# An attention, routing and expert kernel whose first key tile is filled and loaded by other engines, and whose first scores stand behind two groups of decay products

## The chip, the cores and the metric

The kernel runs on one core of a Trainium2 chip. The metric is the device time of one execution, in microseconds (us). TensorE (PE, with its weight loads as PEld), VectorE (DVE), ScalarE (ACT), GpSimd (POOL) and the queue of SyncE (SP) each work through their own list of instructions in order, and semaphores tie the lists together.

## The reference

Three stages follow each other. The first is a gated linear attention with a running maximum, written as a loop over 768 steps for 4 x 8 = 32 heads of width 40:

```python
m_new = np.maximum(f_gate[:, :, t] + m, i_gate[:, :, t])
f_stab = np.exp(f_gate[:, :, t] + m - m_new)
i_stab = np.exp(i_gate[:, :, t] - m_new)
C = f_stab[..., None, None] * C + i_stab[..., None, None] * np.einsum('bhd,bhe->bhde', vt, kt)
n = f_stab[:, :, None] * n + i_stab[:, :, None] * kt
y[:, :, t] = o * np.einsum('bhde,bhe->bhd', C, qt) / np.maximum(np.abs(nq), 1.0)
```

Here `o` is the sigmoid of `o_gate` and `nq` is the product of `n` and `q`. The second stage sends each of the 3072 tokens (320 numbers each) to one of 8 experts, 384 tokens each, greedily by the sorted logits of `x @ w_gate`; an expert is `relu(x @ w1) @ w2` with 1024 inner columns. The third is a gated block over all tokens, `(sigmoid(x @ w_gate) * (x @ w_val)) @ w_out`, with 1536 inner columns.

## The kernel before

The attention is cut into 6 chunks of 128 time steps, and in each chunk the 32 heads go in three sets of 12, 12 and 8. A pair of chunk and set is a step j, so there are 18 steps. Within a step the heads go in groups of four, numbered k; a group is written (j, k) below. For a group, `decay` (lines 221 to 237) multiplies a mask (`tris`, L226) and the running sums of the gates (`GB` by `sel`, L228) into a PSUM tile `pg`, of which there are two, and ScalarE turns it into `ee` by four exponentials (L234). `score` (239 to 246) multiplies keys and queries on TensorE (L245) into `s`, of which there are two as well, and VectorE multiplies `ee` by it (L246). `outp` (L294) multiplies `ee` by the values, `state` (L275 and L283) carries the running matrix on, `comb` and `xout` (L307 to L322) make the output rows `y`.

The key operand of `score` is `KB`, two tiles of 120 partitions x 12 x 128 numbers. Three heads of width 40 share the 120 partitions; each head's column block has keys in its own 40 rows and zeros in the other 80. The zeros are written once, at the start of `setup`, and `load` then writes only the 40 rows of each head, by three transfers (`"k"`, L126).

The start is a chain of its own. `setup` loads the gates of the first 128 steps (L57 on SyncE's queue, L58 on ScalarE's), zeroes the two `KB` tiles on ScalarE, loads queries, values and keys of step 0, then the gates of the other 640 steps (L67, L68), then the operands of step 1. `gates(0, 1)` (151 to 193) makes the running maximum and sums of the first chunk on VectorE; its last line fills the last third of `GB` (L192), on which the first L228 waits. `gates(1, NC)` does the same for the other five chunks: a scan over 640 columns (L156), differences (L158, L170, L159), five scans (L165), and behind them an exponential on ScalarE (`lam`, L185). The sigmoid of the output gate `on` (L139) needs another activation table than the exponentials, so a table load stands before and behind each pair of sigmoids.

The attention is written in the order of `run` and `step`, but it isn't issued so: a scheduler with a model of the engines orders it, and `issue_after` holds an instruction behind a named one. From the routing on (`manual_schedule`) the order is that of the code. While the attention runs, side work splits the weights of the third stage into two parts (L774 to L776 on VectorE, L818 on ScalarE, L819 on GpSimd).

Of the kernel before, what the change touches and what calls it, by code (L numbers as in the profile page):

```python
# [14 lines left out]
AF = mybir.ActivationFunctionType  # L15
# [6 lines left out]
L = 128  # L22
# [8 lines left out]
GK = (3, 3, 2)  # L31
GP = 3 * D
# [8 lines left out]
class Attention:  # L41
# [9 lines left out]
    def setup(self):  # L51
        nc, one, g = self.nc, self.one, self.g
        gp = self.gp
        gt = self.gt = gp.tile([96, 2, S], FT, name="gt")
        gi = [self.a[n].rearrange("b h s -> (b h) s") for n in ("i_gate", "f_gate")]
        for r in range(3):
            nc.sync.dma_start(gt[32 * r:32 * r + 32, 0, :L], gi[0][:, :L])  # L57
            nc.scalar.dma_start(gt[32 * r:32 * r + 32, 1, :L], gi[1][:, :L])  # L58
        self.KN = [one.tile([L, HS, D], FT, name=f"kn{i}") for i in range(2)]
        self.VN = [one.tile([L, HS, 41], FT, name=f"vn{i}") for i in range(NS)]  # L60
        self.KB = [one.tile([GP, 4, 3, L], FT, name=f"kb{i}") for i in range(2)]
        for t in self.KB:
            nc.scalar.activation(t.rearrange("p a r t -> p (a r) t"), g["ident"][:GP, None, :].to_broadcast([GP, 12, L]),
                                 AF.Copy, scale=0.0)
        self.load(0, "qvk")
        for r in range(3):
            nc.sync.dma_start(gt[32 * r:32 * r + 32, 0, L:], gi[0][:, L:])  # L67
            nc.sync.dma_start(gt[32 * r:32 * r + 32, 1, L:], gi[1][:, L:])  # L68
        self.load(1, "kqv")
        g["R"].strict(g["jp"])  # L70
        self.KW = one.tile([L, HS, D], FT, name="kw")
        self.CS = one.tile([GP, NG, 123], FT, name="cs")
        nc.vector.memset(self.KW[:, 8:9], 0.0)
        nc.vector.memset(self.VN[2][:, 8:9], 0.0)
        nc.vector.memset(self.VN[2][:, 8:9, D:], 1.0)
        self.mk = one.tile([GP, 2, 3], FT, name="mk")
        nc.gpsimd.iota(self.mk[:, 0], pattern=[[-D, 3]], base=0, channel_multiplier=1,
                       allow_small_or_imprecise_dtypes=True)
        nc.vector.tensor_scalar(self.mk[:, 1], self.mk[:, 0], 0.0, None, op0=OP.is_ge)
        nc.vector.scalar_tensor_tensor(self.mk[:, 1], self.mk[:, 0], float(D - 1), self.mk[:, 1], op0=OP.is_le,  # L80
                                       op1=OP.mult)
        self.negi = one.tile([L, L], BF, name="negi")
        nc.vector.tensor_scalar(self.negi, g["ident"], NEG, None, op0=OP.mult)
        self.sel = one.tile([96, NB], BF, name="sel")
        it = gp.tile([96, NB], FT, name="it")
        for r in range(3):
            nc.gpsimd.iota(it[32 * r:32 * r + 32], pattern=[[1, NB]], base=0, channel_multiplier=-1,
                           allow_small_or_imprecise_dtypes=True)
        nc.vector.tensor_scalar(self.sel, it, 0.0, None, op0=OP.is_equal)
        self.m = gp.tile([96, S + 1], FT, name="m")  # L90
        self.G = gp.tile([96, S], FT, name="G")
        self.zero = gp.tile([96, 1], FT, name="zero")
        nc.vector.memset(self.zero, 0.0)
        nc.vector.memset(self.m[:, 0:1], NEG)
        self.GT = one.tile([L, NC, 96], FT, name="GT")
        self.GB = one.tile([96, S], BF, name="GB")
        self.LM = one.tile([GP, NG, NC], FT, name="LM")
        self.lam = gp.tile([32, NC], FT, name="lam")
        for _ in self.gates(0, 1):
            pass  # L100
# [10 lines left out]
    def heads(self, s):  # L111
        return s * HS, min(NB, (s + 1) * HS)

    def load(self, j, which):
        nc = self.nc
        c, s = divmod(j, NS)
        h0, h1 = self.heads(s)
        n, ng = h1 - h0, GS[s]
        for w in which:
            if w == "q":  # L120
                self.QT[j] = self.wk.tile([GP, 4, L], FT, name="qT", bufs=3)
                nc.sync.dma_start(self.QT[j][:, :ng], self.a["qt"][c, s, :, :ng])
            elif w == "k":
                for r in range(3):
                    p = slice(D * r, D * r + D)
                    nc.sync.dma_start(self.KB[j % 2][p, :ng, r, :], self.a["kt"][c, s, p, :ng])  # L126
                if c < NC - 1:
                    nc.sync.dma_start(self.KN[j % 2][:, :n], self.a["kn"][c, s, :, :n])
            else:
                nc.sync.dma_start(self.VN[s][:, :n], self.a["vn"][c, s, :, :n])  # L130
                nc.gpsimd.memset(self.VN[s][:, :n, D:], 1.0)
# [89 lines left out]
    def decay(self, j, k):  # L221
        nc = self.nc
        c, s = divmod(j, NS)
        h0 = s * HS + 4 * k
        pg = self.ps.tile([L, 4, L], FT, name="pg", bufs=2)
        nc.tensor.matmul(pg, self.g["R"].tris, self.negi[:, None, :].to_broadcast([L, 4, L]), start=True, stop=False)  # L226
        for h in range(4):
            nc.tensor.matmul(pg[:, h, :], self.sel[:, h0 + h:h0 + h + 1].to_broadcast([96, L]),  # L228
                             self.GB[:, c * L:(c + 1) * L], start=False, stop=(h == 3))
        ee = self.wk.tile([L, 4, L], FT, name="ee", bufs=7)  # L230
        ins, n = self.behind
        with self.tc.issue_after(ins) if n else nullcontext():
            for h in range(4):
                e = nc.scalar.activation(ee[:, h, :], pg[:, h, :], AF.Exp, bias=self.GT[:, c, h0 + h:h0 + h + 1])  # L234
        self.lastexp = e.ins
        self.behind[1] = max(0, n - 1)
        self.W[j, k] = ee

    def score(self, j, k):
        nc = self.nc  # L240
        ee = self.W[j, k]
        s = self.ps.tile([L, 4, L], FT, name="s", bufs=2)
        for h in range(4):
            a, r = divmod(4 * k + h, 3)
            nc.tensor.matmul(s[:, h, :], self.KB[j % 2][:, a, r, :], self.QT[j][:, a, :], start=True, stop=True)  # L245
        nc.vector.tensor_mul(ee, s, ee)  # L246
# [119 lines left out]
    def run(self, rt, fn):  # L366
        with self.tc.tile_pool(name="a_gate", bufs=1) as self.gp:
            self.setup()
            self.kw(0)
            for k in range(GK[0]):  # L370
                self.decay(0, k)
                self.score(0, k)
            gend = self.gend
            g1 = self.gates(1, NC)
            for k in range(GK[1]):
                self.decay(1, k)
            self.step(0, lambda n: [next(g1, 0) for _ in range(2 * n)])
            for _ in g1:
                pass
            self.step(1, lambda n: None)  # L380
            self.setup2()
            self.lambdas()
        with self.tc.tile_pool(name="a_conv", bufs=1) as cv:
            with self.tc.issue_after(gend):
                rt.consts(cv)
            side = fn.prep_moe2(cv)
            for j in range(2, NC * NS + 1):
                self.step(j, lambda n: [next(side, 0) for _ in range(n)])
            for _ in side:
                pass  # L390
# [363 lines left out]
class Ffn:  # L754
# [24 lines left out]
    def prep_moe2(self, wk):  # L779
# [20 lines left out]
        for t in todo[:2]:  # L800
            load(t)
# [440 lines left out]
```

## Time and profile before

| what | value |
|---|---|
| median of three runs | 851.53 us (850.21 to 854.12) |
| the profiled execution | 853.9 us, of which its span is 852.1 us |
| PE busy | 800.9 us, 94% of the span |
| DVE, ACT, POOL busy | 519.4, 334.9 and 230.2 us |
| mean granted TensorE clock | 0.973 of full speed |

The span begins with the first instruction and ends with the last; the 1.8 us beside it lie around the program. A row of a timeline gives the start and the length of a group of like instructions, the engine, the line, the tiles (out<-in) and in brackets how long the engine had sat idle before and what ended that. The attention fills the first 192 us, the routing the next 30, and the experts and the gated block the rest.

### The profile page before, as it was taken

Reading aid. Unit: us, or ns where it says so; the run is one execution under the profiler, and the core shown is the slowest. Engines: PE = TensorE matmul, PEld = TensorE weight load, DVE = VectorE, ACT = ScalarE, POOL = GpSimd, SP = SyncE. Lnnn points to the kernel's source line nnn. Section 1 sums busy time; section 2 is a strip of 40 time slices with the busy share of each in tenths; the row PEclk is TensorE's granted clock in tenths of the full one; section 3 lists DMA queues with packets and bytes.
Section 4 is the critical chain, followed back from the end, with each engine's and each line's share of the span. In section 5 each row is a group of like instructions: output and inputs, shape, how many; then the busy total and the mean of one; then the engine's idle time right before and its main releaser. Section 6 shows DMA issues by size and latency. Waiting matters only on the chain.

```text
span 852.1 us, 15713 instructions
## 1 busy us (share of the span) xinstructions
PE 800.9 (94%) x6049; PEld 761.2 (89%) x6049; DVE 519.4 (61%) x1381; ACT 334.9 (39%) x751; POOL 230.2 (27%) x253
## 2 busy tenths in 40 slices
PE   6888899994799999999999999999999999999996
PEld 5787888893599999999999999999999999999996
DVE  7689989856576576656565665566566652352321
ACT  5565697620342342252334224322522342252321
POOL 2144544410210270081026005400810270072001
PEclk9898999996699999999999999999999999999998
DMA  6586676410400410310051005002200400320000
GB/s 184 172 264 204 209 237 210 133 44 32 132 29 2 144 40 1 104 58 24 2 145 37 3 2 159 24 1 83 78 24 2 144 32 8 94 67 24 1 1 23
DMA packets 40949, 67.64 MB, mean 79 GB/s; under 512 B 5066, under 2 KB 29386, under 8 KB 40874
## 3 DMA queue, kind: packets, MB, share of 16 engines
q1 hardware_dynamic: 38426, 58.72, 22.7%
q0 software_dynamic: 2304, 7.87, 2.8%
q8 instruction: 47, 0.77, 0.4%
q14 instruction: 28, 0.23, 0.1%
q10 hardware_dynamic: 144, 0.05, 0.0%
HBM read 58.76 MB, written 7.86 MB: 78 GB/s over the span
## 4 chain that ended last, share of the span: by engine, by line
PE 72%; DVE 2%; DMA 1%; ACT 0%; issue 0%; POOL 0%; POOLq 0%; ACTq 0%; DVEq 0%
PE mm L1003 8%; PE mm L1025 8%; PE mm L1004 8%; PE mm L1005 8%; PE mm L1010 5%; PE mm L1009 5%; PE ac L1129 5%; PE ac L1131 5%; PE ac L1130 5%; PE ac L1042 3%; PE ac L1044 3%; PE ac L1043 3%; PE rp L611 3%; PE ac L1048 1%; DMA xg<-xd,ix 1%; PE ac L1047 1%
## 5 line engine op out<-in xcount | busy, mean ns | idle before, releaser
L1003 PE MATMUL mm<-yh,mh 128*128 128x384 f32 x384 | 134.0, 349 | 0.0
L1004 PE MATMUL mm<-yh,ml 128*128 128x384 f32 x384 | 129.3, 337 | 0.0
L1005 PE MATMUL mm<-yl,mh 128*128 128x384 f32 x384 | 129.3, 337 | 0.0
L963 POOL DMA_INDIRECT xg<-xd,ix x24 | 23.6, 985 | 371.7 <-DVE scr L730 274.8
L1105 DVE TENSOR_TENSOR gl<-gf,gh 128x384 fp32r<-128x384 f32 x96 | 77.6, 808 | 38.9 <-ACT gh L1111 38.7
L1098 ACT ACTIVATE sg<-mm 128x384 f32<-128x384 f32 x96 | 47.1, 490 | 135.7 <-PE mm L1010 133.7
L1111 ACT ACTIVATE gh<-gf 128x384 fp32r<-128x384 f32 x96 | 50.2, 523 | 109.0 <-DVE gf L1110 109.0
L1129 PE MATMUL ac<-oh,gh 128*128 128x320 f32 x282 | 90.6, 321 | 0.0
L1110 DVE TENSOR_TENSOR gf<-sg,mm 128x384 f32<-128x384 f32 x96 | 52.7, 549 | 60.0 <-ACT sg L1098 59.3
L1131 PE MATMUL ac<-oh,gl 128*128 128x320 f32 x282 | 87.4, 310 | 0.7 <-DVE gl L1105 0.7
L1130 PE MATMUL ac<-ol,gh 128*128 128x320 f32 x282 | 87.4, 310 | 0.0
L1033 ACT ACTIVATE gh<-mm 128x384 fp32r<-128x384 f32 x64 | 31.3, 491 | 115.9 <-PE ac L1048 52.7
L1003 PEld LDWEIGHTS mm<-yh,mh 128*128 128x128 f32 x384 | 72.6, 189 | 0.2 <-DVE xl L944 0.2
L1004 PEld LDWEIGHTS mm<-yh,ml 128*128 128x128 f32 x384 | 72.7, 189 | 0.0
L1005 PEld LDWEIGHTS mm<-yl,mh 128*128 128x128 f32 x384 | 72.3, 188 | 0.0
L1010 PE MATMUL mm<-pad,mr 128*128 128x384 f32 x192 | 64.9, 338 | 0.0
L1009 PE MATMUL mm<-y,m 128*128 128x384 f32 x192 | 64.6, 336 | 0.0
L245 PE MATMUL s<-qT,kb 120*128 120x128 f32 x384 | 57.2, 293 | 2.5 <-DVE ee L246 1.7
L245 PEld LDWEIGHTS s<-qT,kb 120*128 120x128 f32 x384 | 50.6, 203 | 8.5 <-DVE GT L183 4.3
L234 ACT ACTIVATE ee<-pg,GT 128x128 f32<-128x128 f32 x192 | 53.7, 381 | 11.4 <-PE pg L228 9.9
L294 PE MATMUL po<-vn,ee 128*128 128x123 f32 (+2 forms) x384 | 52.6, 287 | 4.3 <-DVE ee L246 4.2
L1034 DVE SCALAR_TENSOR_TENSOR gl<-mm,gh 128x384 fp32r<-128x384 f32 x64 | 34.6, 551 | 33.9 <-ACT gh L1033 33.4
(295 smaller groups left out, 1898.2 us busy)
## 6 DMA issues: line engine op xcount, KB each, us to landing
ws<-in_moe_w_dram SPq DMA_DIRECT2D x15, 480.0 KB
ws<-in_moe_w_dram SPq DMA_DIRECT2D x14, 512.0 KB
ws<-in_moe_w_dram SPq DMA_DIRECT2D x18, 256.0 KB
on<-in_on_dram SPq DMA_DIRECT2D x6, 640.0 KB
xd<-y SPq DMA_DIRECT2D x24, 160.0 KB
st<-in_moe_w_out_dram SPq DMA_DIRECT2D x12, 320.0 KB
st<-in_moe_w_gate_dram SPq DMA_DIRECT2D x8, 384.0 KB
st<-in_moe_w_val_dram SPq DMA_DIRECT2D x8, 384.0 KB
```

Source lines behind the costliest of these rows:

```text
L234: e = nc.scalar.activation(ee[:, h, :], pg[:, h, :], AF.Exp, bias=self.GT[:, c, h0 + h:h0 + h + 1])
L245: nc.tensor.matmul(s[:, h, :], self.KB[j % 2][:, a, r, :], self.QT[j][:, a, :], start=True, stop=True)
L1003: mm(p, wh[:, d, cs], h[:, d], start=(d == 0), stop=False)
L1004: mm(p, wl[:, d, cs], h[:, d], start=False, stop=False)
L1005: mm(p, wh[:, d, cs], l[:, d], start=False, stop=False)
L1009: mm(p, w2[:, cs], x[2], start=False, stop=False)
L1010: mm(p, wr[:, c2], self.pad[z], start=False, stop=True)
L1025: mm(p, (self.al if t == 1 else self.ah)[:, d, cs], x[t // 2][:, d], start=(d == 0 and t == 0), stop=False)
L1105: nc.vector.tensor_tensor(gl, hs[f - 1][0], hs[f - 1][1].bitcast(FT), op=OP.subtract)
L1129: mm(o, gh[:, ts], self.oh[:, k], start=(k == 0), stop=False)
L1130: mm(o, gh[:, ts], self.ol[:, k], start=False, stop=False)
L1131: mm(o, gl[:, ts], self.oh[:, k], start=False, stop=(k == 11))
```

## The change

Two engines take over the zero fills: VectorE zeroes the first `KB` tile and GpSimd the second. `load` gets an optional engine for the key transfers, and the first call passes ScalarE, whose queue then issues the three key transfers of step 0; in that call keys (with the `kn` rows) come first, then queries, then values. `decay` returns its last matmul. In `run`, the groups (0, 0) and (0, 1) of decay products come first, and all scores of step 0, with the decay group (0, 2), are held behind the last matmul of group (0, 1).

```diff
-        for t in self.KB:
-            nc.scalar.activation(t.rearrange("p a r t -> p (a r) t"), g["ident"][:GP, None, :].to_broadcast([GP, 12, L]),
-                                 AF.Copy, scale=0.0)
-        self.load(0, "qvk")
+        nc.vector.memset(self.KB[0], 0.0)
+        nc.gpsimd.memset(self.KB[1], 0.0)
+        self.load(0, "kqv", nc.scalar)
...
-    def load(self, j, which):
+    def load(self, j, which, keng=None):
...
-                    nc.sync.dma_start(self.KB[j % 2][p, :ng, r, :], self.a["kt"][c, s, p, :ng])
+                    (keng or nc.sync).dma_start(self.KB[j % 2][p, :ng, r, :], self.a["kt"][c, s, p, :ng])
...
-            nc.tensor.matmul(pg[:, h, :], self.sel[:, h0 + h:h0 + h + 1].to_broadcast([96, L]),
+            mm = nc.tensor.matmul(pg[:, h, :], self.sel[:, h0 + h:h0 + h + 1].to_broadcast([96, L]),
                              self.GB[:, c * L:(c + 1) * L], start=False, stop=(h == 3))
...
+        return mm.ins
...
-            for k in range(GK[0]):
-                self.decay(0, k)
-                self.score(0, k)
+            self.decay(0, 0)
+            mm = self.decay(0, 1)
+            with self.tc.issue_after(mm):
+                self.score(0, 0)
+                self.decay(0, 2)
+                for k in range(1, GK[0]):
+                    self.score(0, k)
```

The scheduler places the whole attention anew, so the order also differs at many places behind the start. Lines of the changed program stand one lower from L66 to L238 (L228 is L227), as before up to L369, and four higher behind that.

The first place is the start of TensorE's list. Before, eight score products of two groups (`kb_99` is the first key tile) stand ahead of the first products of `sel` and `GB`:

```order
L226 MATMUL pg<-negi,tris 128x512
L182 MATMUL tr<-ident,gt 128x96
L245 MATMUL s<-qT,kb_99 128x128 x8
L228 LDWEIGHTS sel
L228 MATMUL pg<-GB,sel 128x128
...
L275 MATMUL pic<-vn_96,kw 120x123 x4
```

With the change it reads:

```order
L225 MATMUL pg<-negi,tris 128x512
L181 MATMUL tr<-ident,gt 128x96
L227 LDWEIGHTS sel
L227 MATMUL pg<-GB,sel 128x128
...
L245 MATMUL s<-qT,kb_99 128x128 x8
L275 MATMUL pic<-vn_96,kw 120x123 x3
```

The eight products of `sel` that complete two `pg` tiles now stand ahead of the eight scores.

The second place is on TensorE too, some 25 us into the program, where the mask product of group (3, 0) stands. It needs a `pg` tile that is free only when the exponentials of group (2, 0) are done. Before, it stands ahead of the scores of group (1, 2) (`kb_100` is the second key tile) and of the first eight value products of step 1 (`vn_97`):

```order
L182 MATMUL tr<-ident,gt 128x96 x4
L226 LDWEIGHTS tris
L226 MATMUL pg<-negi,tris 128x512
L245 MATMUL s<-qT,kb_100 128x128 x4
L294 MATMUL po<-vn_97,ee 128x123 x8
```

With the change these rows read:

```order
L245 MATMUL s<-qT,kb_100 128x128 x4
L294 MATMUL po<-vn_97,ee 128x123 x8
L275 MATMUL pic<-vn_97,kw 120x123
L245 MATMUL s<-qT,kb_99 128x128
L225 LDWEIGHTS tris
L225 MATMUL pg<-negi,tris 128x512
```

Scores and value products have moved ahead of the mask product of group (3, 0), and the four transposes of the gates ahead of them all.

The third place is the start of SyncE's queue. Before:

```order
L130 DMA vn_96<-in_vn_dram 128x492
L128 DMA kn_94<-in_kn_dram 128x480
L67 DMA gt<-in_i_gate_dram 32x640
L126 DMA kb_99<-in_kt_dram 40x4x128 x3
L68 DMA gt<-in_f_gate_dram 32x640
L67 DMA gt<-in_i_gate_dram 32x640
```

With the change:

```order
L127 DMA kn_94<-in_kn_dram 128x480
L121 DMA qT<-in_qt_dram 120x512
L129 DMA vn_96<-in_vn_dram 128x492
L66 DMA gt<-in_i_gate_dram 32x640
L67 DMA gt<-in_f_gate_dram 32x640
```

The three key transfers have left this queue, and all six transfers of the later gates (`gt`) follow directly on the operands of step 0. On ScalarE's list the three key transfers stand behind its own three gate transfers and ahead of the first table load, and the exponential `lam` of the five later chunks stands behind 12 exponentials where it stood behind 20; the sigmoids stand behind 24 exponentials in both.

## Rows read from the trace of the kernel before

**Rows 1.** The page: span, and granted TensorE clock in 40 equal slices.
```profile
span 852.1 us, 15713 instructions
PEclk9898999996699999999999999999999999999998
```

**Rows 2.** Who waited for whom on PE, 0 to 230 us: total us, times, longest.
```profile
PE pg L226 <- ACT ee L234: 6.1, 4, 4.2
```

**Rows 3.** Timeline of the start: start us, us, engine line op out<-in xcount [idle before <-releaser].
```profile
0.84 0.09 DVE L73 MEMSET kw<- 128x40 f32 x1 [0.84 <-PEq L1229]
...
0.94 0.06 DVE L94 MEMSET m<- 96x1 f32 x1
...
1.82 0.16 POOL L105 MEMSET wgt<- 128x80 f32 x1
...
3.46 2.86 ACT L63 ACTIVATE kb<-ident 120x1536 f32<-120x1536 f32 x2
...
3.65 0.48 DVE L156 TENSOR_TENSOR_SCAN m<-gt,m 96x128 f32<-96x128 f32 x1 [1.42 <-DMA gt<-in_f_gate_dram]
...
4.97 2.62 SPq L126 DMA_DIRECT2D kb<-in_kt_dram  x3
...
7.81 0.90 DVE L192 CAST GB<-G 32x128 bf16<-32x128 f32 x1
7.84 4.03 PE L245 MATMUL s<-qT,kb 120*128 120x128 f32 x16 [0.84 <-ACT GT L184]
...
9.55 0.42 SPq L68 DMA_DIRECT2D gt<-in_f_gate_dram  x1
...
11.58 1.55 DVE L156 TENSOR_TENSOR_SCAN m<-gt,m 96x640 f32<-96x640 f32 x1 [1.88 <-DMA gt<-in_f_gate_dram]
...
11.70 0.61 PE L228 MATMUL pg<-GB,sel 96*128 96x128 bf16 x8
...
12.13 5.26 ACT L234 ACTIVATE ee<-pg,GT 128x128 f32<-128x128 f32 x20 [4.60 <-PE pg L228]
```

**Rows 4.** The same view, 15 to 30 us.
```profile
15.38 0.38 PE L226 MATMUL pg<-negi,tris 128*128 128x512 bf16 x1 [0.43 <-ACT ee L234]
...
16.40 1.16 PE L245 MATMUL s<-qT,kb 120*128 120x128 f32 x8 [0.42 <-DVE ee L246]
...
17.25 0.83 SPq L135 DMA_DIRECT2D on<-in_on_dram  x2
...
19.16 0.21 ACT L185 ACTIVATE lam<-G 32x5 f32<-32x5 f32 x1 [1.77 <-DVE G L165]
...
24.82 0.49 PE L182 MATMUL tr<-ident,gt 96*128 96x96 f32 x4
...
25.70 1.27 ACT L139 ACTIVATE on<-on 128x1280 f32<-128x1280 f32 x1 [0.90 <-DMA on<-in_on_dram]
...
26.99 1.28 ACT L234 ACT_TABLE_LOAD   x1
...
28.29 1.14 ACT L234 ACTIVATE ee<-pg,GT 128x128 f32<-128x128 f32 x4
...
29.48 0.59 PE L226 MATMUL pg<-negi,tris 128*128 128x512 bf16 x1 [4.16 <-ACT ee L234]
```

**Rows 5.** Busy us by stretch (times in brackets are instructions), granted clock, DMA share, GB/s.
```profile
8.00:12.00 4.00, 4.00 (x22) 3.71 (x23) 2.05 (x15) 0.00 (x0) 0.63 (x1) 1.00 0.46 140
...
30.00:31.00 1.00, 1.00 (x7) 1.00 (x6) 0.00 (x0) 0.84 (x4) 0.01 (x1) 0.50 0.78 287
...
35.00:36.00 1.00, 1.00 (x8) 0.91 (x7) 0.00 (x0) 0.00 (x0) 0.00 (x0) 0.76 0.96 309
...
60.00:80.00 20.00, 16.58 (x121) 15.19 (x120) 19.93 (x41) 11.04 (x37) 9.84 (x11) 0.83 0.65 197
```

**Rows 6.** Timeline again: the end of the cold stretch, and a later stall.
```profile
38.00 0.61 PE L228 MATMUL pg<-GB,sel 96*128 96x128 bf16 x8
...
74.31 2.07 PE L294 MATMUL po<-vn,ee 128*128 128x123 f32 x8 [2.54 <-DVE ee L246]
```

## The prediction

> **What bounds the kernel now.** I read the page first. Span and clock slices [rows 1] say that TensorE runs at full clock from about 240 us on, where the order of work is the code's own and this change touches nothing. What can move lies in the attention, the first 192 us, where the clock slices dip for the first time in the second slice (21 to 43 us). So I asked who waits for whom on TensorE up to 230 us. One wait stands out: the mask product of a decay group waits for exponentials, 6.1 us in four waits, the longest 4.2 us [rows 2]. The timeline places it: TensorE finishes the gate transposes at 25.3 us and resumes at 29.48 [rows 4]. ScalarE is what ends it, with a chain of its own: the second transfer of `on` lands at 25.70, its sigmoid takes 1.27, the table goes back for 1.28, and four exponentials run from 28.29 for 1.14 [rows 4]. Behind the wait the granted clock is 0.50, the lower of the two levels (1.2 GHz), up to the stretch from 35 to 36 us, where it is 0.76 [rows 5]. So the idle time is paid twice, once as waiting and once as slow matmuls. Third I read the start [rows 3]. ScalarE, which must make 24 exponentials before those sigmoids, sits idle for 4.60 us until the first decay products come at 12.13, because TensorE works through 16 score passes (4.03 us) first. VectorE waits 1.88 us for the last of the later gates, landed at 11.58. Both delays feed the chain that ends at 29.48.
>
> **The fills.** ScalarE's two fills, 2.86 us [rows 3], go. ScalarE had nothing else to do then, so that alone is worth nothing. VectorE now starts with a fill of 1536 numbers per partition. No row shows one so long. Two small fills, 0.09 us for 40 numbers and 0.06 us for one [rows 3], give a slope of 0.77 ns and a lower bound of 1.2 us; 0.09 us over 40 gives 2.3 ns and an upper bound of 3.5 us. I take 1.4 us, half of ScalarE's 2.86 for two tiles of this very shape, the nearest row in size. Cover: VectorE's small work from 0.84 us ends 1.42 us before the gates land at 3.65 [rows 3], so a fill of 1.4 us just fits, and the chain behind it moves by about 0.2 us (with 3.5 us, by 2.1). GpSimd's fill stands ahead of the small index rows that VectorE needs before the scan; 0.16 us for 80 numbers [rows 3] bounds it at 3.1 us, and with that the chain moves by 1.3 us. I take 0.2 us for both and keep 2.1 as the far end; a gain from these two edits is excluded, since nothing they do starts earlier. The Trainium skill, "VectorE: DVE Perf Modes", section "Zero memsets can be issued as uint32 (trn2)", says that a memset takes one cycle per element whatever the type; at that page's 0.96 GHz this would be an estimate of 1.6 us, the chain would move by 0.4 us in place of 0.2, and the sum below would be 0.2 us smaller. No row here shows a fill of that length.
>
> **The key transfers.** SyncE spends 2.62 us on issuing them from 4.97 [rows 3], and the later gates stand behind. ScalarE now issues them from about 2.3 to 4.9 us, then loads its table (1.28 us, the price of the row at 26.99 [rows 4]), done at 6.2; its first real work on the path is the exponential that released the scores at 7.84 [rows 3]. So nothing is late there. The last gate transfer, issued at 9.55 and landed at 11.58, so 2.0 us later [rows 3], is issued some 3.4 us sooner (2.6 of issue, 0.8 of waiting for the fill) and lands at about 8.2. VectorE is free for it at about 9.8, so the long scan starts about 1.7 us earlier, and so does `lam`, 17.4 in place of 19.16 [rows 4]. The twelve exponentials that now stand behind `lam` then end at about 20.7, as the 24th does now, so no loss comes from the new place of `lam`. The transfers of `on`, issued at 17.25 now [rows 4], have fewer bytes ahead of them: the operands of step 1 leave SyncE 3.4 us sooner. I put the second landing at 23 us or before, and the end of sigmoids and table load at 26.2 in place of 28.29.
>
> The 16 DMA engines are busy 0.46 of the time from 8 to 12 us [rows 5], so the issue and not the movement is what the gates wait for. The Trainium skill, "DMA: Bandwidth & Descriptors", section "Issuing engines are not separate DMA queues", says that all queues run on the same 16 engines and that a second queue saves only the time of issuing. By that rule a full set of engines would land the gates no sooner, and the sum below would be -3.2 in place of -6.2; the share of 0.46 says they are not full.
>
> **TensorE, as a sum up to the eight `sel` products that end at 38.61** [rows 6]. I take away and add, in its own time:
>
> - The wait of 4.16 us before 29.48 [rows 4] goes: minus 4.2. Two things remove it, and either would nearly do. The exponentials come 2.1 us sooner, and four scores and eight value products, which now run behind the wait, stand ahead of it. At full clock those are 3.2 us of work: eight score passes take 1.16 [rows 4], and the 16 value passes, 2.07 for eight at half clock [rows 6], about 1.0 for each eight.
> - The slow clock goes with it. From 29.48 to 35 us it is at half, and 0.76 in the sixth microsecond [rows 5]: 6.0 us at the lower level, of which half is lost: minus 3.0.
> - Three small waits of 0.4 us, two for exponentials and one for a product of VectorE (one of each stands in [rows 4]), go, since ScalarE is ahead by then: minus 1.3.
> - The start is later. `GB` is ready at 8.7 [rows 3], plus 0.2. The eight `sel` products take 0.61 us with the clock up [rows 3] and I allow 0.85; then 16 score passes at their present 4.03 or a little less. They end at 13.6 in place of the 12.3 at which scores and `sel` are done today: plus 1.3.
> - New small waits between 14 and 28 us, for exponentials behind `lam` and for products that VectorE reaches late: none to 2 us; I take plus 1.0.
>
> The sum is -4.2 - 3.0 - 1.3 + 1.3 + 1.0 = -6.2 us. With the fills at their far end it is -4.3, with no new waits -7.2. Behind 40 us everything that is fed by this chain starts that much earlier, the weight splitting on VectorE too. VectorE is the fuller engine there (19.93 of 20 us from 60 to 80 [rows 5]), and since its work begins earlier its end does too; I carry the gain through in full. The profiled execution took 853.9 us, of which 852.1 is span [rows 1]; it would be 847.7. That is 2.4 us above the median of 851.53, so the median should come out at 845.3.
>
> **The rivals.**
>
> *More or fewer stalls behind 40 us.* The scheduler orders the whole attention anew, and there is a second stall in the trace: TensorE waits 2.54 us for a product of VectorE until 74.31 [rows 6], and the clock falls to a mean of 0.83 from 60 to 80 us [rows 5], which is 6.8 us at the lower level, 3.4 lost. Such a stall costs about 5.9 us. If the new order avoids it, the time is 845.3 - 5.9 = 839.4. If it makes one more, 851.2. The slower rival is two more of them, at places between 40 and 190 us where a product of scores now stands behind weight splitting on VectorE: -6.2 + 11.8 = +5.6, so 857.1. It decides from the second wait of TensorE over 2.5 us on. For it speaks that VectorE has no slack there; against it, that the trace has only one such wait in 150 us.
>
> *The gates land no sooner*, since the key transfers and the gate transfers share the 16 engines. Then `lam` stays at 19.16, twelve exponentials behind it end at 22.5, and TensorE waits for them for 2 to 3 us more: 848.3. The share of 0.46 [rows 5] speaks against it.
>
> *The gain is used up.* If VectorE's stretches behind 40 us are held by transfers that come no sooner, the earlier start only makes a longer wait there: 851.5. Against it: the transfers are issued behind scores and value products that come sooner themselves.
>
> **How the numbers follow.** The forecast itself has 0.46 (its own range 843 to 848, by the fills and the new waits), one stall fewer 0.12, gates no sooner 0.10, gain used up 0.08, one stall more 0.12, two more 0.12. A run of this kernel can tell about 0.5%, 4.3 us, from no change; the border is 847.3 and 855.8. Of the forecast's chance 0.42 lies below 847.3. So faster is 0.42 + 0.12 = 0.54, within 0.5% is 0.04 + 0.10 + 0.08 + 0.12 = 0.34, slower 0.12. The range from 838.5 to 853.5 leaves out the slower case and a little at the other end.
>
> **What would show it.** Right: first exponentials near 9.6 us, the long scan near 9.9, `lam` near 17.4, no wait of TensorE over 1.5 us up to 30 us, granted clock at 1.00 from 30 to 36 us, and the eight `sel` products of today's 38.00 (two groups of four) done near 32. Wrong: a fill on VectorE of 2.5 us or more, `on` landing at 25 us or later, or a fresh wait of over 2.5 us behind 40 us with the clock at 0.50 behind it. If the first 40 us come out as worked out and the total doesn't, the later order has taken it back.

## The result, and the profile after

The changed kernel takes 845.29 us (median of 7 runs, 843.58 to 848.44), against 851.53 of the kernel before in the same comparison (7 runs, 850.21 to 856.22). The ratio is 0.9918, with a 95% interval of 0.9893 to 0.9943. The forecast was 845.3. The total was right; one of the steps to it was wrong, and three of its terms were wrong in size. The profiled execution took 846.5 us, 844.7 of them span, 7.4 us less than the 852.1 of [rows 1].

The page of the changed kernel, span and granted clock in 40 slices: the dips of the second and fourth slices are gone; the tenth and eleventh are the routing, as before.

```profile
span 844.7 us, 15715 instructions
...
PEclk9999999995799999999999999999999999999999
```

Who waited for whom on TensorE from 0 to 230 us (total us, times, longest): the row that answers to [rows 2] has 2.4 us in place of 6.1, the longest 1.8 in place of 4.2. The wait of 2.9 us for GpSimd is new.

```profile
PE pic L275 <- POOL vn L130: 2.9, 1, 2.9
...
PE pg L225 <- ACT ee L233: 2.4, 3, 1.8
```

The timeline of the start, beside [rows 3]: start us, us, engine, line, operation, tiles, and in brackets the idle time before and what ended it. (All lines have moved up by one: L226 is now L225.)

```profile
1.06 1.37 POOL L63 MEMSET kb<- 120x1536 f32 x1
1.15 1.34 DVE L62 MEMSET kb<- 120x1536 f32 x1 [1.15 <-PEq L1233]
2.52 3.00 ACTq L125 DMA_DIRECT2D kb<-in_kt_dram  x3
3.70 0.48 DVE L155 TENSOR_TENSOR_SCAN m<-gt,m 96x128 f32<-96x128 f32 x1
5.18 0.31 SPq L66 DMA_DIRECT2D gt<-in_i_gate_dram  x1
5.55 1.28 ACT L184 ACT_TABLE_LOAD   x1 [5.55 <-DVE G L164]
8.27 0.90 DVE L191 CAST GB<-G 32x128 bf16<-32x128 f32 x1
8.63 0.31 SPq L67 DMA_DIRECT2D gt<-in_f_gate_dram  x1
9.22 1.01 PE L227 MATMUL pg<-GB,sel 96*128 96x128 bf16 x8 [2.18 <-DVE GB L191]
9.45 0.42 SPq L67 DMA_DIRECT2D gt<-in_f_gate_dram  x1
9.85 2.17 ACT L233 ACTIVATE ee<-pg,GT 128x128 f32<-128x128 f32 x8 [1.86 <-PE pg L227]
10.03 3.19 PE L245 MATMUL s<-qT,kb 120*128 120x128 f32 x16
11.55 1.55 DVE L155 TENSOR_TENSOR_SCAN m<-gt,m 96x640 f32<-96x640 f32 x1 [1.40 <-DMA gt<-in_f_gate_dram]
```

Three things are to be seen. Both fills take 1.4 us, as taken, and the first scan starts at 3.70 in place of 3.65. The first exponentials start at 9.85 in place of 12.13, and scores and `sel` are through at some 13.1 us (10.03 + 3.19, less the overlap of rows), in place of 12.3. But the long scan starts at 11.55, as late as before (11.58): SyncE stands still from 5.49 to 8.63 between two of the gate transfers.

The same view from 16 to 32 us, beside [rows 4 and 6]:

```profile
18.11 0.21 ACT L184 ACTIVATE lam<-G 32x5 f32<-32x5 f32 x1 [2.64 <-DVE G L164]
...
26.04 1.27 ACT L138 ACTIVATE on<-on 128x1280 f32<-128x1280 f32 x1 [1.54 <-DMA on<-in_on_dram]
27.43 1.28 ACT L233 ACT_TABLE_LOAD   x1
27.71 0.39 PE L245 MATMUL s<-qT,kb 120*128 120x128 f32 x2
28.72 2.17 ACT L233 ACTIVATE ee<-pg,GT 128x128 f32<-128x128 f32 x8
29.91 0.38 PE L225 MATMUL pg<-negi,tris 128*128 128x512 bf16 x1 [1.81 <-ACT ee L233]
31.37 0.38 PE L227 MATMUL pg<-GB,sel 96*128 96x128 bf16 x4
```

ScalarE's chain is no earlier, it is later: the second transfer of `on` lands at 26.04 (before: 25.70), the four exponentials start at 28.72 (28.29), and the mask product behind them at 29.91 (29.48). What changed is what TensorE did up to then: it was busy until 28.1 us with scores and value products that stood behind the wait before. So it waits 1.81 us in place of 4.16, and the eight `sel` products that stood at 38.00 (now two groups of four, the second in the last row) are through at 31.75 us in place of 38.61.

Busy us by stretch (PE, PEld, DVE, ACT, POOL with instructions in brackets; granted clock; DMA share; GB/s), beside [rows 5]:

```profile
8.00:12.00 4.00, 2.78 (x17) 2.78 (x17) 2.50 (x16) 2.15 (x8) 1.02 (x1) 1.00 0.32 89
30.00:31.00 1.00, 1.00 (x11) 0.88 (x11) 0.09 (x1) 1.00 (x6) 0.11 (x1) 1.00 0.72 242
35.00:36.00 1.00, 1.00 (x12) 0.87 (x12) 0.97 (x1) 0.95 (x4) 0.00 (x0) 1.00 0.45 138
60.00:80.00 20.00, 17.15 (x143) 16.34 (x142) 17.41 (x38) 14.25 (x36) 7.62 (x9) 0.91 0.80 241
```

In the microsecond from 30 us TensorE does 11 matmuls at a granted clock of 1.00, where it did 7 at 0.50.

Where the 7.4 us of span are: the first normalised output row of the attention (VectorE, the operation of 960 numbers at L322) starts at 35.03 in place of 40.16, so 5.1 us sooner. The first transposes of the experts, where attention and routing are behind, start 8.6 us sooner. The row of each kernel, before and after:

```profile
223.62 0.90 PE L972 MATMUL ac<-ident,xg 128*128 128x128 f32 x3 [1.88 <-DMA xg<-xd,ix]
```

```profile
215.04 0.90 PE L976 MATMUL ac<-ident,xg 128*128 128x128 f32 x3 [2.23 <-DMA xg<-xd,ix]
```

From there to the end, the same code in the same order took 628.5 us before (852.1 - 223.62) and 629.7 now, so 1.2 us of the lead are missing again at the end.

### The profile page after: what moved, and what is told of

The parts are those of the page before. It is cut to its first block, busy times and chain, and to the rows that moved or that the text cites. A ratio compares the mean times of both kernels' runs of the same rounds, so it can differ in the third digit from the quotient of the medians.

```text
span 844.7 us, 15715 instructions
## 1 busy us (share of the span) xinstructions
PE 796.7 (94%) x6049; PEld 758.0 (90%) x6049; DVE 521.6 (62%) x1382; ACT 332.6 (39%) x749; POOL 233.6 (28%) x254
## 4 chain that ended last, share of the span: by engine, by line
PE 74%; DVE 2%; DMA 1%; ACT 0%; issue 0%; POOL 0%; POOLq 0%; DVEq 0%; ACTq 0%
PE mm L1007 8%; PE mm L1029 8%; PE mm L1008 8%; PE mm L1009 8%; PE mm L1014 5%; PE mm L1013 5%; PE ac L1133 5%; PE ac L1135 5%; PE ac L1134 5%; PE ac L1046 3%; PE ac L1048 3%; PE ac L1047 3%; PE rp L615 3%; PE ac L1052 1%; PE ac L1051 1%; DMA xg<-xd,ix 1%
## 5 line engine op out<-in xcount | busy, mean ns | idle before, releaser
L1135 PEld LDWEIGHTS ac<-oh,gl 128*128 128x128 f32 x282 | 53.0, 188 | 0.9 <-DVE gl L1109 0.9
L1133 PEld LDWEIGHTS ac<-oh,gh 128*128 128x128 f32 x282 | 53.4, 189 | 0.0
```

The lines of the kernel that those rows point to most:

```text
L1133: mm(o, gh[:, ts], self.oh[:, k], start=(k == 0), stop=False)
L1135: mm(o, gl[:, ts], self.oh[:, k], start=False, stop=(k == 11))
```

## The experiments

Each was timed in five rounds beside the kernel before, whose median was 851.55 us in the first four and 852.11 in the last four. The edits are cut to their core.

**The new order alone.** The kernel before with the edit of `run` and the returned matmul, and nothing else:

```diff
-            for k in range(GK[0]):
-                self.decay(0, k)
-                self.score(0, k)
+            self.decay(0, 0)
+            mm = self.decay(0, 1)
+            with self.tc.issue_after(mm):
+                self.score(0, 0)
...
```

> Only the new order in run() (two decay groups, then the scores): fills on ScalarE, keys on SyncE's queue as before. Theory A (the gain comes from TensorE's order: scores and value products ahead of the mask product of group (3, 0)): the wait before that product is under 2.5 us in place of 4.16, the granted clock stays at 1.00 from 30 to 36 us, the first row of y (L322 x960) starts near 35.5 us in place of 40.16, and the time is 845 to 847. Theory B (the gain comes from the fills and the key transfers at the start): the wait is 3.5 us or more and the time is 849.5 or more.

Measured: 846.72 us (845.26 to 849.39), ratio 0.9942, interval 0.9917 to 0.9967. Its timeline has the first exponentials at 9.41 us and the wait at the same mask product cut to 1.03 us, though the exponentials behind `on` come at 28.06, hardly sooner than 28.29:

```profile
9.41 2.17 ACT L234 ACTIVATE ee<-pg,GT 128x128 f32<-128x128 f32 x8 [1.86 <-PE pg L228]
...
28.06 1.14 ACT L234 ACTIVATE ee<-pg,GT 128x128 f32<-128x128 f32 x4
...
29.25 0.38 PE L226 MATMUL pg<-negi,tris 128*128 128x512 bf16 x1 [1.03 <-ACT ee L234]
```

The stretch from 30 to 36 us, which was at a granted clock of 0.54 before, is at 1.00. As theory A has it, the order by itself brings most of the gain; the first normalised row starts at 34.91. The first transposes of the experts start at 214.73, as early as in the changed kernel.

**The fills and the transfers alone.** The changed kernel with the old loop in `run`:

```diff
-            self.decay(0, 0)
-            mm = self.decay(0, 1)
-            with self.tc.issue_after(mm):
...
+            for k in range(GK[0]):
+                self.decay(0, k)
+                self.score(0, k)
```

> Only the new fills and the key transfers on ScalarE's queue; run() as before, so the scores of step 0 stand ahead of the first decay products again. Theory A: the start alone moves the last later gate by less than 0.5 us (it lands near 11.5), the first exponentials start near 11.5, and only as much is won as TensorE's order at group (3, 0) changes by itself: 848 to 851. Theory B: nearly the whole gain, 845 to 847.

Measured: 847.95 us (846.17 to 854.75), ratio 0.9962, interval 0.9940 to 0.9984. With the scores in front the keys are late: TensorE waits 3.50 us for their transfer, and the first exponentials come at 12.97, later than the 12.13 before.

```profile
7.67 0.77 PE L245 MATMUL s<-qT,kb 120*128 120x128 f32 x2 [3.50 <-DMA kb<-in_kt_dram]
...
26.51 1.05 PE L294 MATMUL po<-vn,ee 128*128 128x123 f32 x8
29.69 0.38 PE L225 MATMUL pg<-negi,tris 128*128 128x512 bf16 x1 [2.12 <-ACT ee L233]
```

Still the long wait is halved, with exponentials at 28.50 as late as ever: the scheduler, given other starting times, put scores and value products ahead of the mask product here too. So this version has no sooner input, and what it gains goes with the order that came with it; its time lies just below what theory A gave, and its first exponentials are 1.5 us later than theory A had them.

**`on` first, in the kernel before.** The two transfers of `on` are issued ahead of the operands of step 1:

```diff
+        self.load_o(0)
+        self.load_o(1)
         self.load(1, "kqv")
...
-                self.load_o(0)
-                self.load_o(1)
```

> The kernel before, with the two first transfers of on issued ahead of the operands of step 1 and nothing else. If the chain on, sigmoid, table load, exponentials is what TensorE waited 4.16 us for and what let the clock fall: the wait is under 2 us, the clock at 1.00 from 30 to 36 us and the time is 845 to 847, as with the change. If the chain is only the last of several waits that end together: the wait stays over 3 us or another takes its place, and the time is 850 to 852.

Measured: 846.81 us (845.16 to 848.69), ratio 0.9942, interval 0.9923 to 0.9962. Here the order at the start is the old one (first exponentials at 12.47), and the chain on ScalarE is what came sooner:

```profile
19.14 0.21 ACT L187 ACTIVATE lam<-G 32x5 f32<-32x5 f32 x1 [1.41 <-DVE G L167]
...
21.66 2.43 ACT L141 ACTIVATE on<-on 128x1280 f32<-128x1280 f32 x2
24.11 1.28 ACT L236 ACT_TABLE_LOAD   x1
25.40 2.17 ACT L236 ACTIVATE ee<-pg,GT 128x128 f32<-128x128 f32 x8
```

TensorE's longest wait for exponentials up to 60 us is 0.4 us, and the clock from 30 to 36 us is 1.00. An edit that shares no line with the change gives the same gain as the order alone. The wait of 4.16 us with the slow clock behind it is one prize, and either end of it can be pulled. The two ends aren't wholly apart here: the scheduler also put eight score passes (1.06 us from 25.67) ahead of the mask product, which starts at 26.59 without a wait. The larger part is ScalarE's, whose exponentials start 2.9 us sooner (25.40 in place of 28.29).

**`on` first, in the changed kernel.** The same edit on top of the change:

> The changed kernel, with the two first transfers of on issued ahead of the operands of step 1. TensorE's order up to group (3, 0) is the same. If the wait of 1.81 us that is left before the mask product of (3, 0) hangs on the landing of on (26.04 us): both sigmoids run right behind the table load, the exponentials of (2, 0) start near 26 in place of 28.72, the wait is gone, y starts 1.5 us sooner and the time is 843 to 844.5. If the operands of step 1, now 1.28 MB later, become the wait: TensorE stands for them near 17 to 20 us and the time is 846 or more.

Measured: 846.03 us (843.71 to 846.73), ratio 0.9927, interval 0.9900 to 0.9954. The two sigmoids run back to back from 24.22 and the wait falls from 1.81 to 0.65 us. In exchange the queries of step 1 come late:

```profile
20.13 1.16 PE L247 MATMUL s<-qT,kb 120*128 120x128 f32 x8 [1.12 <-DMA qT<-in_qt_dram]
```

ScalarE then waits 1.35 us for TensorE's decay products, until 21.77, and its exponentials behind `on` come at 28.07, not near 26 as expected. The first normalised row starts at 34.38, 0.7 us sooner than in the changed kernel where 1.5 was expected, and the experts' transposes at 214.27, 0.8 sooner. No difference of the whole can be told.

**The keys back on SyncE.** The changed kernel with one argument taken away:

```diff
-        self.load(0, "kqv", nc.scalar)
+        self.load(0, "kqv")
```

> The changed kernel with the first keys issued by SyncE again (the fills and the new order stay). Theory S: ScalarE's transfers bought nothing; their only effects were a table load late by 0.5 us (5.55 us) and a SyncE that waited 3.1 us. Then the sigmoid lam of the first chunk ends earlier or at 6.84 us, the first exponential by 9.7, the last later gate lands at 11.2 to 11.8 as in both kernels, the longest wait of TensorE up to 30 us stays between 1 and 2.5 us, and the time is 844 to 847. Rival K: the queue gave the sooner attention (the remaining transfers left sooner); then this run is 848 or more and the first y row starts at 37 us or later.

Measured: 846.88 us (845.68 to 848.72), ratio 0.9945, interval 0.9927 to 0.9963, which overlaps that of the changed kernel. ScalarE has its table at 3.45 us and the first exponentials start at 8.76, 1.1 us sooner than with the key transfers in front of the table; the long scan is at 11.80, as in all versions so far.

```profile
2.17 1.28 ACT L184 ACT_TABLE_LOAD   x1 [2.17 <-issue]
...
8.76 2.18 ACT L233 ACTIVATE ee<-pg,GT 128x128 f32<-128x128 f32 x8 [1.18 <-PE pg L227]
...
11.80 1.55 DVE L155 TENSOR_TENSOR_SCAN m<-gt,m 96x640 f32<-96x640 f32 x1 [2.05 <-DMA gt<-in_f_gate_dram]
```

By the first normalised row (34.53) this is as good as the changed kernel (35.03). Theory S holds in its time: ScalarE's queue bought nothing that can be measured. One of its signs was missed: TensorE's wait at the mask product is 0.40 us, not 1 to 2.5, so at that place the keys on ScalarE's queue cost something.

**The later gates first.** The changed kernel with the six transfers of L66 and L67 ahead of `load(0, ...)`:

```diff
+        for r in range(3):
+            nc.sync.dma_start(gt[32 * r:32 * r + 32, 0, L:], gi[0][:, L:])
+            nc.sync.dma_start(gt[32 * r:32 * r + 32, 1, L:], gi[1][:, L:])
         self.load(0, "kqv", nc.scalar)
...
```

> The changed kernel with the six transfers of the later gates issued ahead of the first q, k and v. Theory W: the gates were late only because SyncE waited behind the keys before issuing them; then the last lands at 9 us or before, the long scan starts at 9.9 to 10.3 us in place of 11.55, lam comes at 16.5 to 17.4 in place of 18.11, and since TensorE's wait at the mask product hangs on the transfers of on (landing at 26.0), not on lam, the wait stays at 1 to 2.5 us: time 844 to 847. Rival B (bandwidth): the gates land at 11 us or later whatever the order, the scan stays at 11.5. Rival L: lam was the true limit; wait under 0.5 us and time 842 to 844.

Measured: 849.11 us (848.35 to 851.50), ratio 0.9973, interval 0.9961 to 0.9985, clear of the changed kernel's 0.9893 to 0.9943. In the start everything came that the prediction wanted from ScalarE's queue: the long scan at 9.30 and `lam` at 15.61, both without waiting for a transfer, `on` landed before 22.29. Behind 11 us TensorE has no wait for exponentials up to 60 us.

```profile
9.30 1.55 DVE L155 TENSOR_TENSOR_SCAN m<-gt,m 96x640 f32<-96x640 f32 x1
...
15.61 0.21 ACT L184 ACTIVATE lam<-G 32x5 f32<-32x5 f32 x1 [3.06 <-DVE G L164]
...
22.29 2.43 ACT L138 ACTIVATE on<-on 128x1280 f32<-128x1280 f32 x2
```

The first normalised row starts at 34.26, 0.8 us sooner than in the changed kernel, and the one near 103 us 0.8 sooner. By the next, at 137 us, the kernel is 1.7 us behind. In between TensorE itself stands, and then runs slowly; the stretches, and behind them a wait of VectorE that ends with TensorE's late scores:

```profile
104.00:108.00 4.00, 1.85 (x15) 1.43 (x16) 4.00 (x10) 3.06 (x9) 2.19 (x3) 1.00 0.53 171
108.00:112.00 4.00, 4.00 (x24) 4.00 (x23) 3.13 (x9) 3.98 (x13) 0.16 (x1) 0.57 0.87 249
...
113.08 0.69 DVE L246 TENSOR_TENSOR ee<-s,ee 128x512 f32<-128x512 f32 x1 [1.81 <-PE s L245]
```

It is busy 1.85 of the 4 us from 104 (3.29 in the changed kernel), and the granted clock of the next 4 us is 0.57 (1.00). From 140 to 150 us it is 0.83 (1.00). By the arithmetic of the prediction, which counts half of the time at the lower level as lost, each costs 1.7 us. So the gates were late because of where their issue stood, as theory W said. That SyncE's wait was the only reason isn't shown, since this order puts the gates' bytes ahead of the others too. Its wait (1 to 2.5 us) and its time were wrong: the gain of the start was lost 70 us later, where TensorE stood once more and the clock fell. That this is what lost it is read from the trace and wasn't tried.

**Both remedies at once.** The order alone, with `on` behind the operands of step 1; and the kernel of the last experiment with `on` in the same place:

```diff
         self.load(1, "kqv")
+        self.load_o(0)
+        self.load_o(1)
...
```

> The kernel before with the new order of scores and decay products only, and with the two transfers of on moved up to right behind the operands of step 1. Theory P (the prize is one wait with its cold clock, 5 to 7 us in all, and either remedy takes it): on lands by 23.5 us, no wait of TensorE over 1 us up to 30 us, clock 1.00 from 30 to 36, time 844 to 847.5, no better than either remedy alone. Rival Q (the remedies add): 841 to 843.

Measured: 847.56 us (846.02 to 850.76), ratio 0.9947, interval 0.9927 to 0.9966.

> The changed kernel with the later gates issued first and on right behind the operands of step 1. Both inputs of the late exponentials come sooner: lam by 17.4 us, on landed by 23.5. Theory P: TensorE has no wait over 1 us for exponentials up to 30 us, the first y row starts 1 to 2 us sooner than in the changed kernel (35.03), and the time is 842 to 846, the same as the changed kernel within 0.5%, since later stretches are held by VectorE. Rival Q: the start is carried through to the end with interest, 839 to 841.5.

Measured: 849.17 us (847.39 to 851.40), ratio 0.9967, interval 0.9951 to 0.9983. In both, the start is as theory P has it: the longest wait for exponentials up to 60 us is 0.3 and 0.8 us (the latter at 10.36), and the first normalised rows start at 34.34 and 34.48, not the 1 to 2 us sooner than 35.03 that theory P had for the second. In both the lead is lost behind 80 us, again with the clock: from 108 to 114 us it is 0.51 in the first and 0.50 in the second, about 3 us lost in each. In the first a wait of 3.13 us on TensorE stands ahead of it, which is a stall of the kind that the prediction priced:

```profile
107.96 2.07 PE L297 MATMUL po<-vn,ee 128*128 128x123 f32 x8 [3.13 <-DVE t L307]
```

The remedies don't add, so rival Q falls twice. Theory P is only half right: the first run is just above its range, the second 3 us above. It held the prize to be one, but not that a better start could end worse.

A table of the start and the end of the attention, from the profiles (us). Each profile is of one execution; that of the fills and transfers alone is its fastest (846.17), that of the order alone with `on` moved its slowest (850.76).

| kernel | first y row | experts' first transposes | median |
|---|---|---|---|
| before | 40.16 | 223.62 | 851.53 |
| changed | 35.03 | 215.04 | 845.29 |
| order alone | 34.91 | 214.73 | 846.72 |
| fills and transfers alone | 35.38 | 215.34 | 847.95 |
| `on` first, before | 35.79 | 215.31 | 846.81 |
| `on` first, changed | 34.38 | 214.27 | 846.03 |
| keys on SyncE | 34.53 | 214.98 | 846.88 |
| gates first | 34.26 | 217.21 | 849.11 |
| order alone, `on` moved | 34.34 | 220.00 | 847.56 |
| gates first, `on` moved | 34.48 | 217.36 | 849.17 |

All nine versions start the first row 4.4 to 5.9 us sooner than before. How much lead there is at the end of the routing, 3.6 to 9.4 us, doesn't follow from that. What does go with it is the clock: the three versions whose experts start at 217 us or later are the three in which it is below 1.00 between 100 and 120 us (0.91, 0.83 and 0.83). No version tried is measurably better than the changed kernel.

## Why the prediction was right, and which step failed

**Fills: right.** 1.34 us on VectorE and 1.37 on GpSimd; the scan moved by 0.05. The Trainium skill's rule on zero memsets ("VectorE: DVE Perf Modes", "Zero memsets can be issued as uint32 (trn2)") led to an estimate of 1.6 us; the row says 1.34, and the measurement decides. The chain behind was late by more than the 0.2 us allowed, 0.46 at `GB` (8.27 in place of 7.81), for another reason: ScalarE's table load stood behind its three key transfers and began at 5.55, not at 4.9 as worked out.

**The gates and `on` sooner: wrong.** This is the step that failed. "The last gate transfer ... is issued some 3.4 us sooner ... and lands at about 8.2", `lam` at 17.4, the second landing of `on` "at 23 us or before", exponentials behind it at 26.2. They came at 11.55 (the scan that needs the gates), 18.11, 26.04 and 28.72. The issue of the keys left SyncE's list, but not its path. The program's order, with the semaphores that each transfer waits for, shows why:

```
## SP
6 L67 DMA gt<-in_f_gate_dram 32x640 [waits DMAHW5_49]
7 L66 DMA gt<-in_i_gate_dram 32x640 [waits DMAHW6_49]
8 L67 DMA gt<-in_f_gate_dram 32x640 [waits DMAHW7_49]
9 L66 DMA gt<-in_i_gate_dram 32x640 [waits DMAHW0_49]
10 L67 DMA gt<-in_f_gate_dram 32x640 [waits DMAHW1_49]
## ACT
2 L125 DMA kb_99<-in_kt_dram 40x4x128 [waits DVE_49]
3 L125 DMA kb_99<-in_kt_dram 40x4x128 [waits DMAHW1_49]
4 L125 DMA kb_99<-in_kt_dram 40x4x128 [waits DMAHW3_49]
```

Read so, eight completion counters (DMAHW0 to 7) go round over the transfers of both queues, and a transfer waits for the one before it on its counter. So SyncE, between two gate transfers, waited for keys that ScalarE had issued. The row of SyncE's waits in the changed kernel:

```profile
SPq L67 <- DMA kb<-in_kt_dram: 3.1, 1, 3.1
```

The saving of 3.4 us of issue became a wait of 3.1. That the first key transfer, begun at 2.52, held SyncE until 8.63 has to do with movement too. The prediction judged that by the 0.46 from 8 to 12 us [rows 5], and the same stretch now shows 0.32; but the moved transfers run ahead of it, and there the 16 DMA engines are full up to 7 us. The changed kernel, and behind it one row of the kernel with the keys back on SyncE:

```profile
4.00:5.50 1.50, 0.16 (x1) 0.00 (x0) 1.35 (x6) 0.00 (x0) 0.25 (x3) 1.00 1.00 304
5.50:7.00 1.50, 0.38 (x1) 0.21 (x2) 1.02 (x5) 1.44 (x2) 0.00 (x0) 1.00 0.94 263
7.00:8.60 1.60, 0.04 (x1) 0.00 (x0) 1.41 (x6) 0.27 (x2) 0.65 (x2) 1.00 0.64 133
...
7.00:8.60 1.60, 0.51 (x6) 0.46 (x5) 1.49 (x6) 0.22 (x1) 0.71 (x1) 1.00 0.99 314
```

With the keys on SyncE it waited for no key: the six gate transfers were issued one behind the other, the last at 8.97 in place of 9.45, and yet the long scan started at 11.80, with the engines busy 0.99 and 1.04 from 7 to 10 us. Only with the gates issued first, ahead of the other bytes, were they there by 9.30. How much of the delay is the counter's and how much the full engines', no run shows. The Trainium skill ("DMA: Bandwidth & Descriptors", "Issuing engines are not separate DMA queues") says that a second issuing engine saves only the time to initiate. That the gates landed no sooner agrees with where the rule would have ended, and the full engines agree with its reason; but the counter stood in the way as well, and not even the time to initiate was saved: the last gate transfer was issued at 9.45 in place of 9.55.

The rival "the gates land no sooner" was thus the case, at a chance of 0.10, and the share that spoke against it was taken from the wrong stretch. Its price of 848.3 was wrong: it let TensorE wait 2 to 3 us more than the forecast, and TensorE waited 1.8, with the clock staying up.

**The wait of 4.16 us: shrunk, not gone.** "Two things remove it, and either would nearly do." One of them failed; the other, the work standing ahead, left 1.81 us: a gain of 2.4 in place of 4.2. Order alone and `on` alone confirm that either nearly does, with 1.03 us left in the one and no wait at that place in the other.

**The slow clock: right.** It was at 1.00 from 30 to 40 us, so all of the 3.0 came. This is why the mis-sized wait cost so little: in none of the five versions with 0.4 to 2.1 us left at that place did the stretch behind it fall below 1.00.

**The start and the small waits: better than taken.** Scores and `sel` were done at 13.1 in place of 13.6, since the 16 score passes took 3.19 us, not 4.03: plus 0.8 in place of plus 1.3. The waits of 0.4 us went, and the new ones between 14 and 28 us are two, of 0.21 and 0.25 us: about -0.8 for both terms, where the prediction had -1.3 and +1.0.

The sum with these sizes is -2.4 - 3.0 - 0.8 + 0.8 = -5.4, and the first normalised row came 5.1 us sooner. The forecast had -6.2.

**Carrying the gain through in full: right in the end, by things that cancel.** The lead grew from 5.1 to 8.6 us up to the experts. A part is the stall after 60 us: the wait of 2.54 us is now one of 2.85 for GpSimd up to 67.00, with a granted clock of 0.53 from 67 to 69, but the clock from 60 to 80 us is 0.91 in place of 0.83, which by the arithmetic of the prediction is 3.6 us at the lower level in place of 6.8, or 1.6 us gained. VectorE may be another part: from 0 to 160 us it was busy 143.9 us (33.60 + 35.57 + 36.72 + 37.97) against 133.7 before. The rows from 120 us on, before and after:

```profile
120.00:160.00 40.00, 36.10 (x316) 33.32 (x314) 34.24 (x78) 28.92 (x86) 19.17 (x22) 1.00 0.64 206
```

```profile
120.00:160.00 40.00, 37.19 (x331) 34.71 (x330) 37.97 (x90) 28.95 (x88) 21.51 (x28) 1.00 0.64 188
```

Then 1.2 us were lost in the experts. That stretch runs the same code in all versions, and in the ten profiles of the table it took 628.5 to 631.0 us; what sets it within these 2.5 us stays open. And the profiled pair differs by 7.4 us where the medians differ by 6.2. So the agreement of 845.29 with 845.3 is closer than the working deserves: the steps give the first 40 us to within a microsecond, and the rest lay within what the scheduler's new order moves either way. The gates-first kernels are the rival of more stalls at work: a start 0.6 to 0.8 us better, a new slow stretch behind 100 us, and 4 us more at the end. Two of the prediction's own signs of being wrong came true as well, though the time was right: `on` landed at 26.04, behind 25, and the wait of 2.85 us has the clock near 0.50 behind it.

What the fills and ScalarE's transfers add to the order alone stays open: 845.29 against 846.72, with intervals of 0.9893 to 0.9943 and 0.9917 to 0.9967.

## What to carry to other kernels

Where an engine that is late keeps another waiting, look at both ends: the late chain, and the work that the waiting engine could do first; here either alone brought some 5 us, and both together no more. Before a transfer is moved to another queue, read which completion counter each transfer behind it waits for, and how full the DMA engines are in the stretch it moves to: a queue that no longer issues a transfer can still wait for it. And where a scheduler orders what follows, a better start is a new order, which needs a run of its own: nine starts that were 4.4 to 5.9 us sooner ended 2.9 to 6.2 us sooner in the median, and where the lead was lost TensorE had stood and its clock had fallen.

## What the runs showed of the hardware

The fill of 120x1536 numbers took 1.34 us on VectorE and 1.37 on GpSimd, against 1.43 for each on ScalarE before (2.86 for two): three engines, nearly one price. The table load of 1.28 us is started only when the engine's list comes to it, so transfers issued in front delay it: at 5.55 us behind three key transfers, at 2.17 without them. The granted clock fell to about half behind stretches in which TensorE had stood: 0.50 behind the wait of 4.16 us, 0.53 behind one of 2.85, 0.57 behind 4 us with 1.85 busy; behind the wait of 1.81 us it stayed at 1.00. And the 16 score passes of step 0 took 3.19 to 4.21 us in the nine kernels (the one before among them) in which no transfer interrupts them, 1.4 to 1.9 times the 2.2 us that eight of them at 14.52 us (1.11 us) would give for 16, and all with a granted clock of 1.00 in the records. Eight took 1.91 us behind the wait of the kernel before, at 0.50, so the passes of the start are about as long as at the lower level; why they are stays open.
